# Block 0 in two halves on two queues, block 2 and K's weights moved up in the order of the first loads

## The chip, the cores and the metric

The kernel runs on one core of one Trainium2 chip. The time is device time of one execution in microseconds (us), and lower is better. A core has five engines that each run their own list of instructions in order: TensorE (PE: matmuls, and weight loads beside them), VectorE (DVE), ScalarE (ACT), GpSimd (POOL) and SyncE (SP). They wait for one another through semaphores. SP, ACT and POOL also issue DMA transfers, which the core's 16 DMA engines carry out.

## The reference

One input x of 2048 rows (tokens) by 512 columns goes through a layernorm without weights, and the result xn feeds two branches whose outputs are added to x. All tensors are bf16.

```python
def _A_ref(x, wqkv, wo):          # sliding local attention, 32 heads of 16
    qkv = (x @ wqkv).reshape(B, S, 3, H, Dh)   # -> q, k, v
    idx = pos[:, None] - off[None, :]          # 8 positions: s, s-2, ..., s-14
    logits = einsum('bhsd,bhswd->bhsw', q, k[idx]) * Dh ** -0.5   # masked where idx < 0
    o = einsum('bhsw,bhswd->bhsd', softmax(logits), v[idx])
    return o.reshape(B, S, D) @ wo

def _B_ref(x, w_in, w_sp, b_sp, w_out):        # gated MLP, mixed over positions
    z = gelu(x @ w_in)                         # 512 -> 1792
    z1, z2 = z[..., :896], layernorm(z[..., 896:])
    g = einsum('ts,bsf->btf', w_sp, z2) + b_sp[None, :, None]    # w_sp is 2048 x 2048
    return (z1 * g) @ w_out                    # 896 -> 512

xn = layernorm(A_x)
return A_x + _A_ref(xn, A_wqkv, A_wo) + _B_ref(xn, B_w_in, B_w_sp, B_b_sp, B_w_out)
```

## The kernel before

The 2048 rows are handled as 16 blocks of 128 rows, and for the wide matmuls as 4 groups of 512 rows. All tensors in SBUF are slices of one tile, `arena` (bf16), small statistics lie in `fpool` (f32), and PSUM is one tile, `ps`. So the profile names nearly every operand arena, fpool or ps, and the line number tells the operations apart.

**Stages on TensorE.** First come 15 matmuls on constants (`warm0` to `warm14`, line 561; eight of 512 columns and seven of 128), which need no data. Then V (line 666), the second half of B's first product, called z2 (line 770, in two halves of 448 columns), Q and K (line 682), z1 (line 813), g, the mix over positions with w_sp (line 910), a reduction for the logits (line 718), and the output blocks, attention part (line 966) and MLP part (line 975).

**The first blocks.** Blocks 0 and 1 don't wait for their layernorm: VectorE sums the row (`sum0`, line 592) and centres it (`cen0`, line 594), TensorE transposes the centred block (`xTc0_0`, `xTc0_1`, line 578), ACT copies it out of PSUM (line 599), and the factor 1/std (`rstd`, on POOL, line 621) is applied when V and z2 leave PSUM. The statistics (`bnst`, line 603; `bnag`, 605; `vpe`, 609) and the normalised block (`norm`, line 637) follow. Blocks 2 and 3 are normalised and then transposed on TensorE (`xTr`) with a copy on ACT (`xTe`, line 627). All other blocks, and blocks 0 and 1 for Q and K, are transposed by a DMA from `xn` (`xTd`, line 631, on SP). Q and K of the first group of 512 rows (`Q0_0`, `K0_0`, ...) read the transposed blocks 0 to 3.

**Loads.** ACT issues block 0 (`ldx0`, line 541), block 1 (line 514) and the first half of z2's weights for columns 0 to 447 (`ldwin2a0`, 224 KB, line 524). SP issues V's weights in two halves of 256 KB (`ldwv0`, `ldwv1`, line 518), `ldwin2a1` (224 KB), blocks 2 and 3 (128 KB each), `ldwin2b` (448 KB, line 530: z2's weights for the other columns), blocks 4 to 7, Q's weights (`ldq`, 512 KB, line 536), the DMA transposes `xTd0` and `xTd1`, K's weights (`ldk`, 512 KB, line 536), and blocks 8 to 15. A transpose waits on SP for its `norm`; what is behind it on SP waits too.

**What sets the order.** Every operation is a task with the engine, an estimated duration, priority, and what it reads and writes. `Plan.schedule` (line 123) is a list scheduler: it lays all tasks out in time by their estimates and so fixes each engine's list of instructions before the kernel is built. Semaphore waits are then set from reads and writes. Its settings are `tol` (how much later than the earliest task one of better priority may start and still be taken), the assumed DMA bandwidth and latency, `overlap` (subtracted from the time for which a VectorE task holds its engine), and `land`, a table with landing times in ns given for the first loads. All of these only steer the order; nothing at run time depends on them. In addition, lists of names (lines 1006 to 1015) force an order on the tasks named, so the start on TensorE, POOL, SP, VectorE and ACT is written out by hand:

```python
["ldq", "xTd0", "xTd1", "ldk"] + ["ldx%d" % b for b in range(8, NB)],     # SP
("rstd2", "rstd1", "rstd3", "rstd4", "Vw0"),                              # POOL
("sum0", "cen0", "sum1", "cen1", "bnst0", "bnag0", "vpe0", "bnst2", "bnag2", "vpe2", "bnst1",
 "bnag1", "vpe1", "norm2", "bnst3", "bnag3", "vpe3", "norm0", "norm1", "norm3", "bnst4"),   # VectorE
```

On TensorE the list is 12 warm-up matmuls, the transposes of block 0, three more warm-ups, then V0_0, the transposes of block 1, V0_1, V1, z2_0_0, z2_1_0, z2_0_1, xTr2, z2_1_1, V2, xTr3, z2_2, V3, z2_3, Q0_0.

Of the kernel before, what the change touches and what calls it, by code (L numbers as in the profile page):

```python
# [338 lines left out]
def build_kernel(nc, A_x, A_wqkv, A_wo, B_x, B_w_in, B_w_sp, B_b_sp, B_w_out, out, report=False, emit=True):  # L339
# [3 lines left out]
    NB = S // 128  # L343
# [5 lines left out]
    NVS = 4  # L349
    NPB = 3  # L350
    NXT = 4
    NWARM = 15
    x2 = A_x[0]
    o2 = out[0]

# [3 lines left out]
    off = {}  # L359
# [34 lines left out]
    plan = Plan()  # L394

    with ExitStack() as es:
        ar = es.enter_context(nc.sbuf_tensor("arena", [128, AR], BF))
# [4 lines left out]
        def A(name, n, o2_=0):  # L402
            return ar[:, off[name] + o2_: off[name] + o2_ + n]

        def AC(o_, dims):
            return bass.AP(tensor=ar, offset=o_, ap=[[AR, 128]] + [list(d) for d in dims])
# [10 lines left out]
        def P(bk, n, o_=0):  # L417
            return ps[:, bk.col(o_): bk.col(o_) + n]
# [73 lines left out]
        def dma(eng, fn, nbytes, chan, reads=(), writes=(), name="", xbar=False, prio=0.0, after=()):  # L492
            return T(eng, fn, reads=reads, writes=writes, name=name, prio=prio, after=after,
                     dma=dict(chan=chan, nbytes=nbytes, xbar=xbar))
# [12 lines left out]
          writes=["ident"], est=300, name="ident1")  # L507
# [4 lines left out]
        def ld_x(b, eng="sp"):  # L512
            sl = b
            return dma(eng, lambda e: e.dma_start(A("xin", 512, 512 * sl), x2[128 * b:128 * b + 128, :]), 128 * 512 * 2,
                ("xin", sl), writes=[("xin", sl)], name="ldx%d" % b)

        def ld_wv(hf):
            dma("sp", lambda e: e.dma_start(AC(off["wv"] + 1024 * hf, [[512, 2], [1, 512]]),  # L518
                                            A_wqkv[256 * hf:256 * hf + 256, 1024:1536].rearrange("(c p) n -> p c n",
                                                                                               p=128)),  # L520
                256 * 512 * 2, ("wv", hf), writes=[("wv", hf)], name="ldwv%d" % hf)

        def ld_win2a(kh, eng):
            dma(eng, lambda e: e.dma_start(
                AC(off["w_in2"] + 1792 * kh, [[896, 2], [1, 448]]),
                B_w_in[256 * kh:256 * kh + 256, 896:1344].rearrange("(c p) n -> p c n", p=128)),
                256 * 448 * 2, ("w_in2a", kh), writes=[("w_in2a", kh)], name="ldwin2a%d" % kh)
# [7 lines left out]
        def ld_wqk(which, eng):  # L535
# [2 lines left out]
                A_wqkv[:, 512 * which: 512 * which + 512].rearrange("(c p) n -> p c n", p=128)),  # L538
                512 * 512 * 2, ("wqk", which), writes=[("wqk", which)], name="ld%s" % ("qk"[which]))

        dma("act", lambda e: e.dma_start(A("xin", 512), x2[0:128, :]), 128 * 512 * 2, ("xin", 0),
            writes=[("xin0", 0), ("xin0", 1)], name="ldx0")
        ld_x(1, "act")
        ld_win2a(0, "act")
        ld_wv(0)
        ld_wv(1)
        ld_win2a(1, "sp")
        ld_x(2, "sp")
        ld_x(3, "sp")
        ld_win2b()  # L550
        ld_x(4, "sp")
# [5 lines left out]

        bw = plan.bank("warm")
        for wi in range(NWARM):
            n_ = 512 if wi < 8 else 128  # L560
            T("pe", (lambda bw, n_: lambda t: t.matmul(P(bw, n_), ones[:, 0:128], ones[:, 0:n_], start=True,
                                                       stop=True))(bw, n_),
              writes=[bw], est=(427.0 if n_ == 512 else 107.0), name="warm%d" % wi, prio=1000)

        T("act", lambda a: a.activation(Fv("prime", 4), mhalf, ACTF.Gelu_apprx_tanh), reads=["mhalf"],
          writes=["prime"], est=1500, name="actprime", tbl="gelu")
# [263 lines left out]
        for b in range(2, NB):  # L830
# [7 lines left out]
          writes=[("KTpad", c) for c in range(4)], est=170, name="ktpad", prio=2, after=lnr[:8])  # L838
# [164 lines left out]


        byname = {t.name: t for t in plan.tasks}
        for names in (["warm%d" % wi for wi in range(NWARM - 3)] + ["xTc0_0", "xTc0_1"] +
                      ["warm%d" % wi for wi in range(NWARM - 3, NWARM)] +
                      ["V0_0", "xTc1_0", "xTc1_1", "V0_1", "V1_0", "V1_1", "z2_0_0", "z2_1_0", "z2_0_1", "xTr2",
                       "z2_1_1", "V2_0", "V2_1", "xTr3", "z2_2_0", "z2_2_1", "V3_0", "V3_1", "z2_3_0", "z2_3_1", "Q0_0"],
                      ("rstd2", "rstd1", "rstd3", "rstd4", "Vw0"), ["ldq", "xTd0", "xTd1", "ldk"] + ["ldx%d" % b for b in range(8, NB)],  # L1010
                      ("sum0", "cen0", "sum1", "cen1", "bnst0", "bnag0", "vpe0", "bnst2", "bnag2", "vpe2", "bnst1",
                       "bnag1", "vpe1", "norm2", "bnst3", "bnag3", "vpe3", "norm0", "norm1", "norm3", "bnst4"),
                      ["bnst%d" % b for b in range(4, NB)],
                      ("xcT0_0", "xcT0_1", "xcT1_0", "xcT1_1", "Ve0", "xTe2", "Ve1", "z2g0", "xTe3", "z2g1", "Ve2", "z2g2",
                       "z2s0"), ("V10_1", "Q3_3"), ("z2_3_1", "Q0_1"), ("z2_3_1", "Q0_2"), ("z2_3_1", "Q0_3")):
            for n0, n1 in zip(names, names[1:]):
                if byname[n0] not in byname[n1].deps:
                    byname[n1].odeps.add(byname[n0])

        plan.schedule(tol=30.0, dma_bw=270.0, dma_lat=1300.0, overlap=0.0,  # L1020
                      land=dict(ldx0=3580.0, ldx1=4750.0, ldwv0=4100.0, ldwv1=5350.0, ldwin2a0=6550.0, ldwin2a1=6600.0, ldx2=7050.0, ldx3=7400.0,
                                ldwin2b=8650.0, ldx4=9050.0, ldx5=9400.0, ldx6=9750.0, ldx7=10200.0, ldq=11700.0,
                                ldk=15000.0))
        if report:
            print("arena", AR, "fp", FR)
            plan.report()
# [15 lines left out]
def bass_parallel_sum__sliding_local_dilated__mixer_gmlp__prompt_kernel(  # L1042
    nc, A_x, A_wqkv, A_wo, B_x, B_w_in, B_w_sp, B_b_sp, B_w_out, out
):
    build_kernel(nc, A_x, A_wqkv, A_wo, B_x, B_w_in, B_w_sp, B_b_sp, B_w_out, out)
# [28 lines left out]
```

## Time and profile before

| | us |
|---|---|
| median of 3 runs | 237.98 (237.9, 237.98, 239.03) |
| the profiled execution | 238.3 |
| its span, first to last instruction | 237.1 |
| PE busy | 231.5 (98%) |
| DVE busy | 215.8 (91%) |
| ACT busy | 95.2 (40%) |
| POOL busy | 32.1 (14%) |
| DMA, all 16 engines | 44.12 MB, 186 GB/s on average |

The profile is one execution, and its spans are in us from the first instruction. Busy times add up instructions; register, branch and DMA-issuing instructions are not counted. Matmuls overlap: one of 512 columns is shown with 379 ns, but they follow each other every 216 ns, so differences of start times are used where matmuls follow each other. Single matmul records can be missing. A few landing times of the first loads, as time of issue + time from issue to landing:

| load | issued | landed after |
|---|---|---|
| block 0 (ACT) | 0.81 | 2.7 |
| V's weights, halves (SP) | 0.80, 1.32 | 3.2, 4.0 |
| block 1 (ACT) | 1.26 | 3.1 |
| z2's weights, first columns (ACT, SP) | 1.74, 1.82 | 5.3, 5.4 |
| blocks 2, 3 (SP) | 2.33, 2.8 | 5.1, 4.9 |
| z2's weights, other columns (SP) | 3.31 | 5.7 |
| Q's weights (SP) | 6.21 | 5.7 |
| DMA transposes of blocks 0, 1 (SP) | 11.24, 12.6 | 2.9, 2.4 |
| K's weights (SP) | 13.88 | 4.5 |
| block 15 (SP) | 18.0 | 5.0 |

### The profile page before, as it was taken

Reading aid. Unit: us, or ns where it says so; the run is one execution under the profiler, and the core shown is the slowest. Engines: PE = TensorE matmul, PEld = TensorE weight load, DVE = VectorE, ACT = ScalarE, POOL = GpSimd, SP = SyncE. Lnnn points to the kernel's source line nnn. Section 1 sums busy time; section 2 is a strip of 40 time slices with the busy share of each in tenths; the row PEclk is TensorE's granted clock in tenths of the full one; section 3 lists DMA queues with packets and bytes.
Section 4 is the critical chain, followed back from the end, with each engine's and each line's share of the span. In section 5 each row is a group of like instructions: output and inputs, shape, how many; then the busy total and the mean of one; then the engine's idle time right before and its main releaser. Section 6 shows DMA issues by size and latency. Waiting matters only on the chain.

```text
span 237.1 us, 2958 instructions
## 1 busy us (share of the span) xinstructions
PE 231.5 (98%) x1109; PEld 108.5 (46%) x1130; DVE 215.8 (91%) x269; ACT 95.2 (40%) x141; POOL 32.1 (14%) x56
## 2 busy tenths in 40 slices
PE   8998999999999999999999999999999999999996
PEld 3444455555444444444444444444444444444443
DVE  4787989999997899999999999999989998999982
ACT  3496889988986896601113411111111111000000
POOL 1476381401634000000000000000000000000000
DMA  6979869998147239014299999999899866393443
GB/s 205 304 205 259 205 135 197 142 230 187 66 152 249 60 116 115 0 33 144 66 358 230 225 231 185 296 173 316 274 212 271 293 189 195 76 320 118 145 139 129
DMA packets 83117, 44.12 MB, mean 186 GB/s; under 512 B 55440, under 2 KB 82464, under 8 KB 83104
## 3 DMA queue, kind: packets, MB, share of 16 engines
q1 hardware_dynamic: 81600, 41.30, 70.7%
q0 software_dynamic: 800, 2.11, 2.3%
q10 hardware_dynamic: 704, 0.52, 0.7%
q8 instruction: 9, 0.15, 0.2%
q14 instruction: 4, 0.03, 0.1%
HBM read 26.35 MB, written 4.21 MB: 129 GB/s over the span
## 4 chain that ended last, share of the span: by engine, by line
PE 90%; DMA 4%; DVE 3%; issue 1%; SPq 1%; ACT 0%; POOL 0%; DVEq 0%
PE ps L910 41%; PE ps L682 11%; PE ps L813 10%; PE ps L975 10%; PE ps L770 8%; PE ps L966 6%; PE ps L666 4%; DMA arena<-in_A_x_dram 2%; DMA arena<-in_A_wqkv_dram 2%; DVE fpool L603 1%; ACT arena L775 0%; PE ps L718 0%; SPq L518 0%; DVE arena L981 0%; DVE fpool L605 0%
## 5 line engine op out<-in xcount | busy, mean ns | idle before, releaser
L910 PE MATMUL ps<-arena 128*128 128x512 bf16 x439 | 96.6, 379 | 0.5
L910 PEld LDWEIGHTS ps<-arena 128*128 128x128 bf16 x448 | 43.7, 98 | 53.1 <-issue 0.4
L918 ACT ACTIVATE arena<-ps 128x1024 bf16<-128x1024 f32 (+1 forms) x16 | 14.7, 916 | 75.3 <-PE ps L910 75.3
L703 DVE TENSOR_TENSOR arena<-arena 128x4096 bf16<-128x4096 bf16 x16 | 36.5, 2288 | 0.2
L938 DVE TENSOR_TENSOR arena<-arena 128x4096 bf16<-128x4096 bf16 x16 | 36.5, 2284 | 0.0
L941 DVE TENSOR_TENSOR arena<-arena 128x2048 bf16<-128x2048 bf16 (+1 forms) x32 | 30.6, 958 | 1.0
L682 PE MATMUL ps<-arena 128*128 128x512 bf16 x126 | 28.9, 379 | 1.3 <-DMA arena<-in_A_wqkv_dram 1.2
L708 DVE TENSOR_TENSOR arena<-arena 128x4096 bf16<-128x4096 bf16 x12 | 27.5, 2290 | 0.3
L975 PE MATMUL ps<-arena 128*128 128x512 bf16 (+2 forms) x117 | 26.9, 366 | 0.1
L770 PE MATMUL ps<-arena 128*128 128x448 bf16 x128 | 26.0, 352 | 0.0
L813 PE MATMUL ps<-arena 128*128 128x512 bf16 x110 | 24.4, 379 | 0.1
L682 PEld LDWEIGHTS ps<-arena 128*128 128x128 bf16 x128 | 14.3, 113 | 14.7 <-DMA arena<-in_A_wqkv_dram 1.7
L691 ACT ACTIVATE arena<-ps 128x1024 bf16<-128x1024 f32 x16 | 16.3, 1021 | 5.3 <-PE ps L682 5.0
L770 PEld LDWEIGHTS ps<-arena 128*128 128x128 bf16 x128 | 12.4, 98 | 11.7 <-DMA arena<-in_B_w_in_dram 0.2
L975 PEld LDWEIGHTS ps<-arena 128*128 128x128 bf16 x119 | 11.4, 98 | 12.8
L813 PEld LDWEIGHTS ps<-arena 128*128 128x128 bf16 x112 | 10.9, 98 | 13.3 <-ACT arena L819 0.3
L966 PE MATMUL ps<-arena 128*128 128x512 bf16 (+2 forms) x66 | 16.5, 366 | 0.1
L819 ACT ACTIVATE arena<-ps 128x1024 bf16<-128x1024 f32 (+1 forms) x16 | 13.9, 922 | 4.9 <-PE ps L813 4.9
L666 PE MATMUL ps<-arena 128*128 128x512 bf16 x60 | 15.2, 379 | 0.7 <-ACT arena L599 0.3
L780 ACT ACTIVATE arena<-arena 128x896 bf16<-128x896 bf16 x16 | 15.1, 946 | 0.1
L775 ACT ACTIVATE arena<-ps 128x896 bf16<-128x896 f32 x14 | 12.8, 915 | 3.3 <-PE ps L770 3.3
L981 DVE TENSOR_TENSOR arena<-ps,arena 128x512 bf16<-128x512 f32 (+2 forms) x17 | 10.4, 653 | 3.3 <-PE ps L975 2.8
(61 smaller groups left out, 168.8 us busy)
## 6 DMA issues: line engine op xcount, KB each, us to landing
arena<-vscr SPq DMA_DIRECT2D x16, 1024.0 KB, 6.0
arena<-in_A_x_dram SPq DMA_DIRECT2D x30, 128.0 KB, 4.1
vscr<-arena POOLq DMA_DIRECT2D x16, 128.0 KB, 2.3
out_dram<-arena SPq DMA_DIRECT2D x15, 128.0 KB, 2.0
arena<-in_A_wqkv_dram SPq DMA_DIRECT2D x2, 512.0 KB, 5.1
arena<-in_B_w_in_dram SPq DMA_DIRECT2D x1, 896.0 KB, 5.4
arena<-in_B_w_out_dram SPq DMA_DIRECT2D x1, 896.0 KB, 5.0
arena<-arena SPq DMA_TRANSPOSE x34, 2.9
```

The costliest lines, as they stand in the source:

```text
L666: last = t.matmul(P(bk, 512), xTv(b, dc), A("wv", 512, 512 * dc), start=(dc == 0), stop=(dc == 3))
L682: last = t.matmul(P(bk, 512, 512 * which), AC(off["wqk"] + 2048 * which + 512 * dc + c, [[4, 128]]), AC(off["xnT"] + dc * S + 512 * j, [[1 ...
L691: T("act", lambda a: a.activation(AC(qo, [[ko - qo, 2], [1, 512]]), P(bk, 1024).rearrange("p (t n) -> p t n", t=2), ACTF.Copy, scale=0.5), ...
L703: T("dve", (lambda pbv, qb, kb: lambda v: v.tensor_tensor(pbv, qb, kb, ALU.mult))(pbv, qb, kb), reads=rd, writes=[("pb", s_)], est=c_tt(40 ...
L708: T("dve", (lambda av, bv: lambda v: v.tensor_tensor(av, av, bv, ALU.add))(av, bv), reads=[("pb", 1)], writes=[("pb", acc)], est=c_tt(4096 ...
L770: last = t.matmul(P(bk, 448, 512 * hf), xTv(b, dc), AC(off["w_in2"] + 896 * dc + 448 * hf, [[1, 448]]), start=(dc == 0), stop=(dc == 3))
L813: last = t.matmul(P(bk, 512, 512 * i), AC(off["w_in1"] + 896 * dc + 128 * fc, [[1, 128]]), AC(off["xnT"] + dc * S + 512 * j, [[1, 512]]), ...
L910: last = t.matmul(P(bk, 512, 512 * i), AC(off["z2"] + FH * sh + 128 * fc, [[1, 128]]), AC(off["wT%d" % r_] + sh * 512, [[1, 512]]), start= ...
L938: T("dve", lambda v: v.tensor_tensor(tv, tv, av, ALU.mult), reads=[("attn", b)], writes=[("Vs", sv)], est=c_tt(4096), name="pv%d" % b, pri ...
L941: T("dve", (lambda n: lambda v: v.tensor_tensor(A("Vs", n, 4096 * sv), A("Vs", n, 4096 * sv), A("Vs", n, 4096 * sv + n), ALU.add))(n), wri ...
L966: last = t.matmul(P(bk, cn), AC(off["OT"] + 512 * tb + 128 * cc, [[1, 128]]), AC(off["wo"] + 512 * cc + c0, [[1, cn]]), start=(cc == 0), s ...
L975: last = t.matmul(P(bk, cn), AC(off["z1T"] + fc * S + 128 * tb, [[1, 128]]), AC(off["w_out"] + 512 * fc + c0, [[1, cn]]), start=False, sto ...
```

## The change

Block 0 is loaded by two DMAs of 64 rows each, one on ACT and one on SP, where SP's half is ahead of V's weights. Block 2's load moves ahead of `ldwin2a1` on SP. K's weights move ahead of the transposes `xTd0` and `xTd1`, directly behind Q's. `norm0` moves up on VectorE to just behind `vpe2`, and `rstd0` is written to the front of POOL's list. One of the wide warm-up matmuls goes (15 to 14, seven of 512 columns), and four instead of three of the narrow ones stand behind block 0's transposes, ten instead of twelve warm-ups ahead of them. The scheduler's settings change: `tol` 30 to 5, assumed bandwidth 270 to 250, latency 1300 to 1600, `overlap` 0 to 30, and the landing table. The computation is the same.

```diff
--- before.py
+++ after.py
@@ -349,7 +349,7 @@
     NVS = 4
     NPB = 3
     NXT = 4
-    NWARM = 15
+    NWARM = 14
     x2 = A_x[0]
     o2 = out[0]
 
@@ -538,14 +538,16 @@
                 A_wqkv[:, 512 * which: 512 * which + 512].rearrange("(c p) n -> p c n", p=128)),
                 512 * 512 * 2, ("wqk", which), writes=[("wqk", which)], name="ld%s" % ("qk"[which]))
 
-        dma("act", lambda e: e.dma_start(A("xin", 512), x2[0:128, :]), 128 * 512 * 2, ("xin", 0),
-            writes=[("xin0", 0), ("xin0", 1)], name="ldx0")
+        for hf, eng in ((0, "act"), (1, "sp")):
+            dma(eng, (lambda hf: lambda e: e.dma_start(ar[64 * hf:64 * hf + 64, off["xin"]: off["xin"] + 512],
+                                                       x2[64 * hf:64 * hf + 64, :]))(hf),
+                64 * 512 * 2, ("xin0", hf), writes=[("xin0", hf)], name="ldx0_%d" % hf)
         ld_x(1, "act")
         ld_win2a(0, "act")
         ld_wv(0)
         ld_wv(1)
+        ld_x(2, "sp")
         ld_win2a(1, "sp")
-        ld_x(2, "sp")
         ld_x(3, "sp")
         ld_win2b()
         ld_x(4, "sp")
@@ -557,7 +559,7 @@
 
         bw = plan.bank("warm")
         for wi in range(NWARM):
-            n_ = 512 if wi < 8 else 128
+            n_ = 512 if wi < 7 else 128
             T("pe", (lambda bw, n_: lambda t: t.matmul(P(bw, n_), ones[:, 0:128], ones[:, 0:n_], start=True,
                                                        stop=True))(bw, n_),
               writes=[bw], est=(427.0 if n_ == 512 else 107.0), name="warm%d" % wi, prio=1000)
@@ -1003,24 +1005,26 @@
 
 
         byname = {t.name: t for t in plan.tasks}
-        for names in (["warm%d" % wi for wi in range(NWARM - 3)] + ["xTc0_0", "xTc0_1"] +
-                      ["warm%d" % wi for wi in range(NWARM - 3, NWARM)] +
+        for names in (["warm%d" % wi for wi in range(NWARM - 4)] + ["xTc0_0", "xTc0_1"] +
+                      ["warm%d" % wi for wi in range(NWARM - 4, NWARM)] +
                       ["V0_0", "xTc1_0", "xTc1_1", "V0_1", "V1_0", "V1_1", "z2_0_0", "z2_1_0", "z2_0_1", "xTr2",
                        "z2_1_1", "V2_0", "V2_1", "xTr3", "z2_2_0", "z2_2_1", "V3_0", "V3_1", "z2_3_0", "z2_3_1", "Q0_0"],
-                      ("rstd2", "rstd1", "rstd3", "rstd4", "Vw0"), ["ldq", "xTd0", "xTd1", "ldk"] + ["ldx%d" % b for b in range(8, NB)],
-                      ("sum0", "cen0", "sum1", "cen1", "bnst0", "bnag0", "vpe0", "bnst2", "bnag2", "vpe2", "bnst1",
-                       "bnag1", "vpe1", "norm2", "bnst3", "bnag3", "vpe3", "norm0", "norm1", "norm3", "bnst4"),
+                      ("rstd0", "rstd2", "rstd1", "rstd3", "rstd4", "Vw0"),
+                      ["ldq", "ldk", "xTd0", "xTd1"] + ["ldx%d" % b for b in range(8, NB)],
+                      ("sum0", "cen0", "sum1", "cen1", "bnst0", "bnag0", "vpe0", "bnst2", "bnag2", "vpe2", "norm0",
+                       "bnst1", "bnag1", "vpe1", "norm2", "bnst3", "bnag3", "vpe3", "norm1", "norm3", "bnst4"),
                       ["bnst%d" % b for b in range(4, NB)],
-                      ("xcT0_0", "xcT0_1", "xcT1_0", "xcT1_1", "Ve0", "xTe2", "Ve1", "z2g0", "xTe3", "z2g1", "Ve2", "z2g2",
-                       "z2s0"), ("V10_1", "Q3_3"), ("z2_3_1", "Q0_1"), ("z2_3_1", "Q0_2"), ("z2_3_1", "Q0_3")):
+                      ("xcT0_0", "xcT0_1", "xcT1_0", "xcT1_1", "Ve0", "xTe2", "Ve1", "z2g0", "xTe3",
+                       "z2g1", "Ve2", "z2g2", "z2s0"), ("V10_1", "Q3_3"), ("z2_3_1", "Q0_1"), ("z2_3_1", "Q0_2"),
+                      ("z2_3_1", "Q0_3")):
             for n0, n1 in zip(names, names[1:]):
                 if byname[n0] not in byname[n1].deps:
                     byname[n1].odeps.add(byname[n0])
 
-        plan.schedule(tol=30.0, dma_bw=270.0, dma_lat=1300.0, overlap=0.0,
-                      land=dict(ldx0=3580.0, ldx1=4750.0, ldwv0=4100.0, ldwv1=5350.0, ldwin2a0=6550.0, ldwin2a1=6600.0, ldx2=7050.0, ldx3=7400.0,
-                                ldwin2b=8650.0, ldx4=9050.0, ldx5=9400.0, ldx6=9750.0, ldx7=10200.0, ldq=11700.0,
-                                ldk=15000.0))
+        plan.schedule(tol=5.0, dma_bw=250.0, dma_lat=1600.0, overlap=30.0,
+                      land=dict(ldx0_0=2700.0, ldx0_1=3050.0, ldx1=3650.0, ldwv0=4350.0, ldwv1=5250.0, ldwin2a0=6300.0,
+                                ldwin2a1=6850.0, ldx2=5800.0, ldx3=7250.0, ldwin2b=8400.0, ldx4=8750.0, ldx5=9100.0,
+                                ldx6=9450.0, ldx7=9800.0, ldq=11300.0, ldk=12800.0))
         if report:
             print("arena", AR, "fp", FR)
             plan.report()
```

## The prediction

> **What bounds the kernel now.** I read the busy line and the chain of the page first, then TensorE's waits, then the timeline of the first 19 us on every engine, then the landing times of single loads, and last the tail.
>
> The busy line, the chain by engine, and two of TensorE's five waits:
>
> ```profile
> PE 231.5 (98%) x1109; PEld 108.5 (46%) x1130; DVE 215.8 (91%) x269; ACT 95.2 (40%) x141; POOL 32.1 (14%) x56
> PE 90%; DMA 4%; DVE 3%; issue 1%; SPq 1%; ACT 0%; POOL 0%; DVEq 0%
> ...
> PE ps L682 <- DMA arena<-in_A_wqkv_dram: 1.2, 1, 1.2
> ...
> PE ps L666 <- ACT arena L599: 0.3, 1, 0.3
> ```
>
> TensorE is the bound: 231.5 of 237.1 us. Its waits sum to 2.7 us, 0.8 of them before the first matmul. One is large: 1.2 us for K's weights (line 682 is the Q and K projections). After that, only 0.2 us is called a wait. So time comes only from this wait, from starting V earlier, or from new stalls.
>
> The first 19 us, from the timelines (start, length, engine, line, operation, count; in brackets the idle time before and what ended it):
>
> ```profile
> 0.80 0.97 SPq L518 DMA_DIRECT2D arena<-in_A_wqkv_dram  x2
> 0.81 0.42 ACTq L541 DMA_DIRECT2D arena<-in_A_x_dram  x1
> 3.50 0.69 DVE L592 TENSOR_REDUCE fpool<-arena 128x1 f32<-128x512 bf16 x1 [2.31 <-DMA arena<-in_A_x_dram]
> 5.56 0.59 PE L666 MATMUL ps<-arena 128*128 128x512 bf16 x2 [0.28 <-ACT arena L599]
> 7.46 0.69 DVE L603 BATCH_NORM_STATS2 fpool<-arena 128x6 f32<-128x512 bf16 x1 [0.89 <-DMA arena<-in_A_x_dram]
> 7.62 2.43 PE L770 MATMUL ps<-arena 128*128 128x448 bf16 x12
> 9.03 0.58 PEld L770 LDWEIGHTS ps<-arena 128*128 128x128 bf16 x4 [0.18 <-DMA arena<-in_B_w_in_dram]
> 11.24 2.59 SPq L631 DMA_TRANSPOSE arena<-arena  x2
> 13.88 0.58 SPq L536 DMA_DIRECT2D arena<-in_A_wqkv_dram  x1
> 16.25 1.03 PE L682 MATMUL ps<-arena 128*128 128x512 bf16 x4
> 18.45 6.24 PE L682 MATMUL ps<-arena 128*128 128x512 bf16 x27 [1.18 <-DMA arena<-in_A_wqkv_dram]
> 18.74 0.69 DVE L603 BATCH_NORM_STATS2 fpool<-arena 128x6 f32<-128x512 bf16 x1 [1.53 <-DMA arena<-in_A_x_dram]
> ```
>
> Block 0's sum starts at 3.50, V at 5.56, z2 at 7.62. SP's last early load (Q's weights) is issued at 6.21 for 0.43; then SP stands until norm0 lets the first transpose go at 11.24. Only behind both transposes (2.59) does it issue K's weights, at 13.88; they land 4.5 later. Q0_0 runs from 16.25 to 17.28, and TensorE then stands 1.18.
>
> The tail, from the chain and SP's timeline:
>
> ```profile
> 228.75 1.19 SPq L947 DMA_TRANSPOSE arena<-arena  x1
> ...
> 232.76 0.65 PE ps L966 x4
> ```
>
> The last transpose of the attention output is issued at 228.75 and lands 2.45 later (such transposes took 2.4 to 2.5), at 231.2. The block that reads it starts at about 232.6. So VectorE's chain has 1.4 us to spare at the end.
>
> **The change part by part.**
>
> K's weights ahead of the first transposes. They go out at about 7.2 instead of 13.88 (Q's 6.21, plus the extra 0.48 slot on SP, plus 0.5). Q's 512 KB landed at 11.9 (5.7 after issue), and the four loads and Q's ahead of that moved at some 350 GB/s, so another 512 KB takes 1.5 more: K lands near 13.4, against a need at 17.2. The whole 1.18 goes. What is late next: Q0_0 needs both first transposes. In the old order they landed at 14.1 and 15.0 (2.9 and 2.4 after issue). Now their 2 x 1.29 us of issue stands behind one issue of about 0.5, which ends by 7.8, before norm0 is done; their data stands behind K's in the rings. The nearest row: the later transposes at 18.56 and 19.8 landed 5.1 and 4.3 after issue, 0.7 and 1.1 behind the eight loads ahead of them (the last landed at 23.0). By that the first two land at 14.1 and about 14.5 or, if norm1 is no earlier than before, at 15.0. Q0_0 needs them at 16.1, so 1 us is left. Cost 0; without that cover every us late is a us lost.
>
> Loads of blocks 8 to 15 follow the second transpose with no K issue between: 0.6 to 2 us sooner than 14.50. VectorE's 1.53 for block 8 shrinks; TensorE does not wait for it, so 0. But QK1 needs transposes 4 to 7, and the last (issued 23.2, landed 26.1) came just before TensorE's 26.22. Those four follow block 15's load on SP and move forward with it; if that is by only 0.6, 0.6 of the gain is lost there. I take the larger figure, since block 8's load no longer waits for K's issue (0.6) and norm0 and its 1.29 of transpose issue come early.
>
> Block 0 in halves. By the quarter-microsecond windows the engines had moved 127 KB by 2.50 and 256 KB by 3.00; both x0 (128 KB) and V's first weights (256 KB) were out at 0.8, and x0 landed at 3.50, some 0.5 after its share. Alone at the front, its 128 KB would be moved by about 2.5 and land near 3.05 to 3.1. So sum, centring, the first PE transposes and V start 0.42 sooner: 5.14, and V ends at 7.2 instead of 7.62. One warm-up matmul of 0.43 goes; the ten ahead of the transposes end at 0.84 + 7 x 0.427 + 3 x 0.11 = 4.16, in time for 4.3.
>
> But z2 then meets its weights. Their halves landed at 7.05 and 7.17; SP's half now has 128 KB of block 2 ahead (0.4 at 337 GB/s) and an issue 0.96 later: 7.2 to 7.55. z2_0_0 and z2_1_0 take 8 x 0.189 = 1.51, to 8.7 to 9.06. The second half of the weights (w_in2b) landed at 9.02, with 1,920 KB in all through it; the same 1,920 KB stand there after the change. So z2_0_1 starts at 9.02 to 9.06 instead of 9.13. The start is worth **-0.1**, the 0.42 is swallowed. Bounds: the engines' gaps between 2.0 and 2.75 (shares 0.63, 0.82, 0.57) and at 4.5 to 5.0 come to 0.35 us; filled, w_in2b lands by that much earlier: -0.45. If instead landing follows issue, which is 0.48 later for everything behind the half on SP, w_in2b lands at 9.5: +0.37. I take -0.1, because the shares near 1.0 from 2.75 to 10 say bytes set the pace.
>
> DVE and POOL orders. norm0 (0.40) moves ahead of bnst1 and norm2. norm2 ended at 9.88 for a transpose on PE at 9.94. Block 2 lands about 1 us earlier, so the statistics that waited 0.89 at 7.46 start near 6.5, and norm2 ends near 9.5 even with norm0 ahead. rstd0 heads POOL as it did in the trace (6.73). Cost 0; if block 2 came no earlier, 0.4 would go.
>
> New constants for the list scheduler can reorder everything behind. A gain is bounded by the idle left on PE after 18.45, about 0.3; a loss by VectorE slipping (below). With a single wait of 0.2 in 216 us under the old constants, I take 0.
>
> **Sum:** -1.18 - 0.1 = -1.28. The profiled execution took 238.3 (span 237.1 and 1.2 around it); it becomes 237.0 with a span of 235.8. The median of the runs is 0.32 below the profiled one, so 237.98 - 1.28 = **236.7**. With the start's bounds, 236.3 to 237.2. About 0.5% (1.19 us, so 236.8 and 239.2) is what can be told from no change here.
>
> **The rivals.**
>
> The halves buy nothing and cost the slot (w_in2b at 9.5): -1.18 + 0.37 = -0.8, **237.2**. For it: wv0 and every load behind it is issued 0.48 later. Against: the saturated shares. The Trainium skill, DMA: Bandwidth & Descriptors, section Rules for kernel authors, speaks for it: two transfers to disjoint partition halves share the same engines and serialize, so one 128-partition transfer should be used. By that rule alone x0 would land at 3.50 as before; what the trace shows is only that x0 shared the engines with wv0.
>
> The start is kept (w_in2b 0.35 earlier): -1.18 - 0.45 = -1.6, **236.35**. For it: the gaps at 2.0 to 2.75. Against: the loads behind the first need an issue of 0.45 to 0.48 each, and only 128 KB are out at 0.8 instead of 384.
>
> The transposes behind K's weights come late, and Q0_0 or QK1 waits. It decides beyond 1 us late; 1.3 more takes the whole gain: **238.0**. For it: 26.1 against 26.22 at QK1, and a transpose issue that took 2.05 at 21.1 beside loads. Against: all that is ahead of them on SP ends earlier.
>
> Slower: the new order makes VectorE late for TensorE. VectorE is 91% busy; its 269 operations are now each counted 30 ns shorter, 8 us in all, and it has 1.4 us to spare at the end, when both chains move by the same amount. One 4096-wide product (2.28) put ahead of block 15's chain takes 0.9 of the gain; slower by 0.5% needs 1.4 + 1.28 + 1.19 = 3.9. A block's whole chain (2.28 + 1.95 + 0.43 = 4.66) costs 4.66 - 1.4 - 1.28: +2.0, **240.0**. Against: VectorE waited only 6 to 7 us after 18.6, mostly for ACT, PE and loads that move too.
>
> **How the numbers follow.** Forecast 0.46 (236.5 to 237.0, of that 0.28 beyond 0.5%); halves cost 0.14 (same); start kept 0.13 (faster); transposes late 0.08 (same); VectorE late 0.19 (slower). Faster 0.28 + 0.13 = 0.41; same 0.18 + 0.14 + 0.08 = 0.40; slower 0.19. The range starts at 235.9 (the start kept, the 0.3 of idle gone, and the 0.1 by which the two lower runs differ) and reaches to 239.4, halfway into the last case, so that about 0.12 is left out. Cases of both signs hold chance; the forecast's own range is 236.3 to 237.2.
>
> **What would show it.** Block 0's sum near 3.1; V near 5.15; z2_0_1 still at 9.0 to 9.1, with TensorE's wait for w_in now visible; K's weights issued near 7.2 and landed by 13.5; Q0_0 near 16.1 and K right behind it without idle; block 8's load issued near 12.4. It is wrong if Q0_0 waits for a transpose, if z2_0_0 starts after 7.7, or if the waits of TensorE after 20 us, 0.2 now, exceed 1 us (lines 718, 966 and 975 are where VectorE could be late).

## The result and the profile after

| | before | after |
|---|---|---|
| median, us (22 runs each) | 238.06 (237.6 to 239.03) | 237.03 (236.63 to 239.47) |
| after / before | | 0.9959, 95% interval 0.9948 to 0.9971 |
| the profiled execution, us | 238.3 | 236.64 |
| its span, us | 237.1 | 235.4 |

The change gains 0.98 us (238.06 x 0.0041; by the interval 0.7 to 1.2). The interval excludes zero, but the gain is below the 0.5% (1.19 us) under which the prediction counts a time as unchanged. The two profiled executions differ by more, 1.66 us, because the one of after is among the quickest of its kernel and the one of before is 0.24 above its median.

From the page of after, the busy line and the chain by engine:

```profile
PE 232.0 (99%) x1129; PEld 108.5 (46%) x1129; DVE 208.0 (88%) x269; ACT 94.7 (40%) x141; POOL 34.6 (15%) x56
PE 96%; DMA 2%; DVE 1%; ACTq 0%; issue 0%; DVEq 0%
```

All of TensorE's waits in after (engine, line, what it waited for, us in total, times, longest):

```profile
PE ps L563 <- PEq L1063: 0.8, 1, 0.8
PE ps L580 <- DVE arena L596: 0.3, 1, 0.3
PE ps L668 <- ACT arena L601: 0.2, 1, 0.2
```

K's wait of 1.2 us is gone, and none has come in its place: all three lie ahead of the first V matmul. The chain is now 96% TensorE. VectorE counts 7.8 us less for the same 269 operations.

The start and the end of after, from the timelines (columns as in the prediction; where a view ends inside a row of matmuls, its last line counts only those up to there):

```profile
0.80 0.58 SPq L542 DMA_DIRECT2D arena<-in_A_x_dram  x1
0.81 0.57 ACTq L542 DMA_DIRECT2D arena<-in_A_x_dram  x1
1.43 0.84 ACTq L514 DMA_DIRECT2D arena<-in_A_x_dram  x1
3.39 0.69 DVE L594 TENSOR_REDUCE fpool<-arena 128x1 f32<-128x512 bf16 x1 [2.19 <-DMA arena<-in_A_x_dram]
5.01 0.69 DVE L594 TENSOR_REDUCE fpool<-arena 128x1 f32<-128x512 bf16 x1 [0.55 <-DMA arena<-in_A_x_dram]
5.45 0.59 PE L668 MATMUL ps<-arena 128*128 128x512 bf16 x2 [0.22 <-ACT arena L601]
6.51 0.98 SPq L536 DMA_DIRECT2D arena<-in_A_wqkv_dram  x2
7.78 2.43 PE L772 MATMUL ps<-arena 128*128 128x448 bf16 x12
8.45 3.86 SPq L633 DMA_TRANSPOSE arena<-arena  x2
12.35 4.03 SPq L514 DMA_DIRECT2D arena<-in_A_x_dram  x8
16.11 7.07 PE L684 MATMUL ps<-arena 128*128 128x512 bf16 x32
23.02 2.43 PE L772 MATMUL ps<-arena 128*128 128x448 bf16 x12
25.29 4.91 PE L684 MATMUL ps<-arena 128*128 128x512 bf16 x22
...
221.10 1.19 SPq L949 DMA_TRANSPOSE arena<-arena  x1
```

Block 0's two halves are issued at 0.80 and 0.81, each for longer than the whole block was before (0.42). Q and K go out together from 6.51. Q0_0 starts at 16.11 and K follows as one piece of 32 matmuls. Then come **12** z2 matmuls, where before has 8, and the next group's Q and K (called QK1 from here on) at 25.29. The last transpose of the attention output goes out at 221.1 instead of 228.75. Two lines of before from the same view, not shown yet:

```profile
24.52 1.68 PE L770 MATMUL ps<-arena 128*128 128x448 bf16 x8
26.22 1.03 PE L682 MATMUL ps<-arena 128*128 128x512 bf16 x4
```

**One account for all kernels.** Matmuls overlap, so I count starts. From Q0_0 to the z2 behind it takes 8.27 us before (16.25 to 24.52) and 6.91 after (16.11 to 23.02): K's wait cost 1.36, not the 1.18 that is marked as idle. A z2 matmul takes 0.189, so QK1 could start 1.51 behind the eight of before; it starts 1.70 behind, 0.19 lost and not marked as a wait. After takes 2.27 for its 12, which is 12 x 0.189: nothing lost. Together 1.55 is gained behind Q0_0. The profiled time minus the start of Q0_0 says the same, 222.05 before and 220.53 after, 1.52 less. Here is that account for every kernel that ran (us; "K" is Q0_0 to z2 less 6.91, "QK1" the excess over 0.189 a matmul):

| kernel | Q0_0 starts | lost at K | lost at QK1 | profiled time less Q0_0's start | median | ratio to before |
|---|---|---|---|---|---|---|
| before | 16.25 | 1.36 | 0.19 | 222.05 | 238.06 | |
| after | 16.11 | 0 | 0 | 220.53 | 237.03 | 0.9959 |
| e1 | 16.02 | 0 | 0.87 | 221.35 | 237.78 | 0.9973 [0.9958, 0.9987] |
| e2 | 16.01 | 0 | 0 | 220.52 | 236.67 | 0.9934 [0.9919, 0.9949] |
| e3 | 16.37 | 0 | 0 | 220.53 | 236.89 | 0.9955 [0.9936, 0.9974] |
| e4 | 16.24 | 0 | 0 | 221.80 | 238.33 | 1.0009 [0.9995, 1.0022] |
| e5 | 16.81 | 0 | 0 | 220.68 | 237.17 | 0.9962 [0.9947, 0.9977] |
| e6 | 16.45 | 1.27 | 0.43 | 222.21 | 238.57 | 1.0016 [1.0007, 1.0025] |
| e7 | 16.33 | 0 | 0.57 | 221.10 | 237.49 | 0.9983 [0.997, 0.9997] |
| e8 | 16.22 | 0 | 0 | 220.80 | 237.17 | 0.996 [0.9948, 0.9972] |
| e9 | 16.41 | 0.78 | 0.68 | 222.04 | 237.39 | 0.9976 [0.996, 0.9991] |
| e10 | 16.30 | 0 | 0 | 220.57 | 236.94 | 0.996 [0.9948, 0.9973] |
| e11 | 16.00 | 0 | 0 | 220.50 | 236.69 | 0.9946 [0.9934, 0.9958] |
| e12 | 16.08 | 0 | 0 | 220.53 | 236.81 | 0.9952 [0.994, 0.9965] |

Six of the kernels without a stall behind Q0_0 agree within 0.07 in the fifth column, and before, e1, e6, e7 and e9 come within 0.05 of 220.53 when the losses of the two columns ahead of it are taken off. e4, e5 and e8 don't fit that. Part of it lies outside the span: in all 25 runs of these three the time is 1.39 to 1.54 above the span, in every run of the other kernels whose span is on record 1.17 to 1.35. Span less Q0_0's start is 219.29 in after and e5, 219.28 in e8 and 220.36 in e4, so e5 and e8 lose nothing inside it and e4 has a loss of its own, of 1.07 (below). Why these three kernels have more outside the span stays open. Ratios are against runs of before beside them, whose medians were 238.2 (e1 to e4), 238.08 (e5 to e8) and 237.85 (e9 to e12).

### The profile page after: what moved, and what is told of

It reads as the page before. It is cut to its first block, busy times and chain, and to the rows that moved or that the text cites. A ratio compares the mean times of both kernels' runs of the same rounds, so it can differ in the third digit from the quotient of the medians.

```text
span 235.4 us, 2986 instructions
## 1 busy us (share of the span) xinstructions
PE 232.0 (99%) x1129; PEld 108.5 (46%) x1129; DVE 208.0 (88%) x269; ACT 94.7 (40%) x141; POOL 34.6 (15%) x56
## 4 chain that ended last, share of the span: by engine, by line
PE 96%; DMA 2%; DVE 1%; ACTq 0%; issue 0%; DVEq 0%
PE ps L912 41%; PE ps L684 12%; PE ps L772 10%; PE ps L815 10%; PE ps L977 10%; PE ps L968 6%; PE ps L668 6%; DMA arena<-in_A_x_dram 2%; PE ps L720 1%; DVE arena L983 0%; PE ps L580 0%; DVE fpool L594 0%; ACTq L542 0%; DVE arena L596 0%; DVEq L319 0%
## 5 line engine op out<-in xcount | busy, mean ns | idle before, releaser
L684 PEld LDWEIGHTS ps<-arena 128*128 128x128 bf16 x128 | 14.4, 113 | 13.2 <-ACT arena L672 0.4
L983 DVE TENSOR_TENSOR arena<-ps,arena 128x512 bf16<-128x512 f32 (+2 forms) x17 | 11.1, 658 | 9.1 <-PE ps L977 8.7
L923 DVE TENSOR_TENSOR arena<-arena 128x1024 bf16<-128x1024 bf16 (+1 forms) x16 | 10.0, 623 | 9.3 <-ACT arena L920 9.2
L772 PEld LDWEIGHTS ps<-arena 128*128 128x128 bf16 x128 | 12.4, 98 | 11.7
```

The source lines that it names most:

```text
L684: last = t.matmul(P(bk, 512, 512 * which), AC(off["wqk"] + 2048 * which + 512 * dc + c, [[4, 128]]), AC(off["xnT"] + dc * S + 512 * j, [[1 ...
L772: last = t.matmul(P(bk, 448, 512 * hf), xTv(b, dc), AC(off["w_in2"] + 896 * dc + 448 * hf, [[1, 448]]), start=(dc == 0), stop=(dc == 3))
```

## The experiments

In all but e4 to e8 the orders of the base kernel are kept and only the tasks named are moved, by editing each engine's planned list. In e4 to e8 changed settings lay the plan out anew. No kernel leaves work out. `...` in an edit stands for lines left out, which only number the tasks anew or define `behind`, a helper that puts one task directly behind another on its engine.

**e1: K's weights first, alone.** Before, with one task moved on SP.

```diff
+        sp_ = plan.order["sp"]
+        lk = byname["ldk"]
+        sp_.remove(lk)
+        sp_.insert(sp_.index(byname["ldq"]) + 1, lk)
...
```

> The kernel before with one move: K's weights are issued directly behind Q's, ahead of the two transposes; every other engine keeps its order of before. Theory (the gain of the change is K's wait): K0_0 follows Q0_0 without idle, and as Q0_0's first matmul to z2 of block 4 took 8.27 us before and 6.91 after, 1.2 to 1.35 us go: 236.7 to 236.9 against 238.06. The first transpose still waits for norm0 at 11.2, so block 8's load is issued at about 13.9. Rival (the halves or the new order carry at least half of the gain): 0.5 us or less, 237.5 or more.

Measured: 237.78, ratio 0.9973: about half of what was expected (three of its twelve runs, 236.67 to 236.76, came as expected). K's wait is gone, but TensorE stands one step later. From e1's waits of TensorE:

```profile
PE ps L682 <- DMA arena<-arena: 0.7, 1, 0.7
```

And from its timelines of TensorE, then SP:

```profile
16.02 7.07 PE L682 MATMUL ps<-arena 128*128 128x512 bf16 x32
22.93 1.68 PE L770 MATMUL ps<-arena 128*128 128x448 bf16 x8
25.31 1.03 PE L682 MATMUL ps<-arena 128*128 128x512 bf16 x4 [0.70 <-DMA arena<-arena]
...
10.87 2.65 SPq L631 DMA_TRANSPOSE arena<-arena  x2
13.56 5.30 SPq L514 DMA_DIRECT2D arena<-in_A_x_dram  x8
18.91 5.12 SPq L631 DMA_TRANSPOSE arena<-arena  x4
```

Transposes 4 to 7 are issued from 18.91. TensorE now reaches the z2 ahead of QK1 1.59 sooner (22.93 against 24.52), and QK1 waits for the last of them: 2.38 between starts where 1.51 would do. Of the 1.36 won at K, 0.87 - 0.19 goes here. Moving K's weights is therefore not the whole change.

**e2: the change without the halves.** After, with block 0 whole on ACT and no half on SP.

```diff
+        byname["ldx0_0"].fn = lambda e: e.dma_start(A("xin", 512), x2[0:128, :])
+        gone = byname["ldx0_1"]
+        plan.order["sp"].remove(gone)
+        plan.tasks.remove(gone)
+        for t in plan.tasks:
+            t.deps.discard(gone)
+            t.odeps.discard(gone)
```

> The changed kernel with block 0 in one DMA on ACT; every engine's order as after, only SP's half is gone. Theory (the halves are worth nothing): block 0's sum starts at 3.4 to 3.5 instead of 3.39, block 1 lands at 4.4 to 4.6 instead of 5.0, V starts within 0.15 us of 5.45, z2 starts earlier than 7.78; time as after within 0.2 us (237.0). Rival (the halves are the start's gain): V starts 0.4 later or more, and the time goes up by 0.3 or more, 237.3 to 237.5.

Measured: 236.67, ratio 0.9934, not slower without them; the time is 0.4 below after's, where 0.2 either way was expected. The start of e2 by its timeline:

```profile
0.80 0.43 ACTq L1028 DMA_DIRECT2D arena<-in_A_x_dram  x1
1.26 0.45 ACTq L514 DMA_DIRECT2D arena<-in_A_x_dram  x1
3.56 0.69 DVE L594 TENSOR_REDUCE fpool<-arena 128x1 f32<-128x512 bf16 x1 [2.37 <-DMA arena<-in_A_x_dram]
4.65 0.69 DVE L594 TENSOR_REDUCE fpool<-arena 128x1 f32<-128x512 bf16 x1
5.62 0.59 PE L668 MATMUL ps<-arena 128*128 128x512 bf16 x2 [0.22 <-ACT arena L601]
7.67 2.43 PE L772 MATMUL ps<-arena 128*128 128x448 bf16 x12
```

Whole, block 0 is summed 0.17 later than in after (3.56, a little past the 3.4 to 3.5 expected), but block 1's sum starts 0.36 sooner, so V starts 0.17 later and z2 0.11 earlier. Q0_0 starts 0.10 earlier.

**e3: K's weights back behind the transposes.** After, with `ldk` moved behind `xTd1`.

```diff
+        sp_ = plan.order["sp"]
+        lk = byname["ldk"]
+        sp_.remove(lk)
+        sp_.insert(sp_.index(byname["xTd1"]) + 1, lk)
...
```

> The changed kernel with K's weights issued behind both transposes again; every other engine's order as after. Theory (what counts is only whether K lands before about 17.0): the second transpose's issue ends at 12.3 because norm0 and norm1 are early now, K's weights go out at 12.35 and land 4.5 later at 16.8, just in time: no wait or up to 0.2 us, 236.9 to 237.3. Rival (the place behind the transposes is what costs): K waits about 1.2 again and the time is 238.0 to 238.3.

Measured: 236.89, ratio 0.9955, as after. With `norm0` early both transposes are issued from 8.56, K's weights go out at 12.45 instead of 13.88 and land 4.3 later, at 16.8, in time. So within after's order, the early `norm0` is enough to bring K's weights in time, here about 0.5 us ahead of need; in before's order it was not in the one trace there is (e9).

**e4: the old settings.** After, with the scheduler's old settings; lists and landing table stay new.

```diff
-        plan.schedule(tol=5.0, dma_bw=250.0, dma_lat=1600.0, overlap=30.0,
+        plan.schedule(tol=30.0, dma_bw=270.0, dma_lat=1300.0, overlap=0.0,
```

> The changed kernel with the scheduler's settings of before (tol 30, bandwidth 270, latency 1300, overlap 0); loads and lists of names as after. Theory (the order behind the start is worth nothing while TensorE never waits): within 0.3 us of after, 236.8 to 237.3; VectorE has less to spare at the end (some 1 to 2 us). Rival (the new settings carry part of the gain): 237.5 or more, with waits of TensorE after 20 us.

Measured: 238.33, ratio 1.0009: the whole gain is lost, against 0.9955 of e3, which ran beside it, though K doesn't wait. The theory fell, and the rival held. From e4's waits of TensorE:

```profile
PE ps L968 <- DMA arena<-arena: 0.9, 1, 0.9
```

And from its timelines near the end, VectorE's three lines first, then one of SP and one of TensorE:

```profile
220.63 1.88 DVE L983 TENSOR_TENSOR arena<-ps,arena 128x512 bf16<-128x512 f32 x3
224.21 0.69 DVE L983 TENSOR_TENSOR arena<-ps,arena 128x512 bf16<-128x512 f32 x1 [1.70 <-PE ps L977]
224.82 2.28 DVE L940 TENSOR_TENSOR arena<-arena 128x4096 bf16<-128x4096 bf16 x1
...
229.57 1.19 SPq L949 DMA_TRANSPOSE arena<-arena  x1
...
232.09 0.82 PE L968 MATMUL ps<-arena 128*128 128x384 bf16 x4 [0.89 <-DMA arena<-arena]
```

VectorE stands 1.70 in its own queue for an output add (line 983, the add of block 11, `fin11_0`) that needs TensorE's result, and the chain of block 15 stands behind it. Its transpose goes out at 229.57, and TensorE's first block that reads it starts 2.57 after the matmuls ahead of it instead of 1.51: 1.06 of the 1.27 that e4 has over after in the table (the rest lies outside the span).

**e5, e6, e7: which setting?** I took `overlap`. e5 is after with `overlap` 0 (the first pair of lines); e6 is before with `overlap` 30 (the second pair); e7 is e6 with e1's move.

```diff
-        plan.schedule(tol=5.0, dma_bw=250.0, dma_lat=1600.0, overlap=30.0,
+        plan.schedule(tol=5.0, dma_bw=250.0, dma_lat=1600.0, overlap=0.0,
...
-        plan.schedule(tol=30.0, dma_bw=270.0, dma_lat=1300.0, overlap=0.0,
+        plan.schedule(tol=30.0, dma_bw=270.0, dma_lat=1300.0, overlap=30.0,
```

> The changed kernel with one setting of before, overlap 0 instead of 30; the other settings stay. Theory (the overlap setting alone decides at the end: with 0 the scheduler puts output adds that wait for TensorE ahead of the last steps of block 15's attention chain, and TensorE then waits for that chain): VectorE about 215 us busy again, TensorE waits 0.5 to 1 us at line 968 near 231, 237.6 to 238.3. Rival (it is tol, or the assumed bandwidth and latency): 236.8 to 237.2, no wait at line 968.

> The kernel before with overlap 30 instead of 0, nothing else. Theory (the order behind the start is worth something only where TensorE gets there earlier): K's wait stays at about 1.2, VectorE about 208 us busy and done with block 15's chain some 10 us sooner, but the time moves by 0.3 us at most: 237.8 to 238.2. Rival (the better order of VectorE's list is worth the gain by itself): 237.3 or less.

> The kernel before with both: K's weights ahead of the first transposes, and overlap 30. K first alone gave 0.5 to 0.6 us. Theory (K's wait of 1.34 us goes, part of it is lost again at QK1 behind the transposes of blocks 4 to 7, since norm0 is as late as before, and part at the end, where the old order makes TensorE wait for VectorE): the part at the end comes back; 236.9 to 237.4, a wait of up to 0.7 at line 682 stays. Rival (nothing was lost at the end, the runs of K first alone differ for another reason): 237.7 to 237.9.

Measured: e5 237.17 (0.9962), no wait at line 968, and VectorE at 207.9 us: `overlap` alone isn't it, that theory fell. e6 238.57 (1.0016): VectorE's busy time drops from 215.8 to 207.7 us and the time doesn't drop at all, with K's wait still there; it is even 0.4 longer, a little more than expected. e7 237.49 (0.9983), just above its theory's range: no tail wait, but 0.41 marked at QK1 (0.57 between starts). The account says that e1 had lost nothing at the tail either (221.35 less its 0.87 at QK1 is 220.48); the loss under the old order sits at QK1.

**e8: the one add, with the old settings.** e4 with `fin11_0` moved on VectorE behind the chain of block 15. On SP the store and the load that hang on that add go behind the transpose.

```diff
...
+        behind("dve", "fin11_0", "pvc15")
+        behind("sp", "ldxr15", "OTd15")
+        behind("sp", "st11_0", "OTd15")
...
```

> The changed kernel with all the settings of before, as in the run that took 238.3, and by hand one output add (block 11) moved on VectorE from ahead of block 15's product to behind block 15's chain, with its store and the load of block 15's x moved behind block 15's transpose on SP. Theory (this one add, which waits 1.7 us for TensorE, makes the whole difference): no wait at line 968, 237.0 to 237.4. Rival (the old settings cost elsewhere, or VectorE has too much work as such): 237.9 or more.

Measured: 237.17, ratio 0.996, as after, and no wait at line 968. e8's VectorE timeline where e4 waited:

```profile
220.60 1.88 DVE L983 TENSOR_TENSOR arena<-ps,arena 128x512 bf16<-128x512 f32 x3
222.40 2.28 DVE L940 TENSOR_TENSOR arena<-arena 128x4096 bf16<-128x4096 bf16 x1
```

The product follows the three adds at once, 2.42 sooner. One 0.69-us operation in the wrong place had cost e4 its gain. SP's order was not what held e4's transpose: it went out at 229.57, when VectorE's chain had just ended (229.12 + 0.43).

**e9, e10: `norm0` early, alone and taken back.** e9 is before with `norm0` directly behind `vpe2` on VectorE (the first line); e10 is after with `norm0` back behind `vpe3` (the second).

```diff
...
+        behind("dve", "norm0", "vpe2")
...
+        behind("dve", "norm0", "vpe3")
...
```

> The kernel before with one move on VectorE: norm0 directly behind vpe2. Loads, SP's list (K's weights behind both transposes), settings and all else as before. Theory (norm0, late, holds SP: it decides when everything behind the first transpose goes out): first transpose at about 8.2, second at about 11.2, K's weights at 12.5 and landed by 16.9, block 8's load at 13.1, so K0_0 waits 0.2 us at most and QK1 little: 236.8 to 237.3. Rival (K's place in SP's list is what counts): K0_0 still waits 0.8 or more, 237.6 or more.

> The changed kernel with norm0 moved back on VectorE to behind vpe3; K's weights stay ahead of the transposes. Theory (as above): no wait for K, but the first transpose at about 11, block 8's load at about 13.8, transposes 4 to 7 about 1.5 later than in the changed kernel, and QK1 waits 0.4 to 1.2 for the last of them: 237.5 to 238.0. Rival (with K ahead, norm0's place is free): 237.0, no wait at line 684.

Measured: e9 237.39 (0.9976), between theory and rival and about what e1 gains. In its trace K's weights go out at 12.64, but land only 5.3 later, at 17.9. e9's waits:

```profile
PE ps L682 <- DMA arena<-in_A_wqkv_dram: 0.6, 1, 0.6
PE ps L682 <- ACT arena L780: 0.5, 1, 0.5
```

That execution took 238.45, the longest of its eight runs (from 236.81), so the row shows what can still go wrong there, not the usual size. e10 236.94 (0.996): no stall, although its transposes stand as late as e1's; its theory fell, and the rival held. e10's timelines of SP and TensorE:

```profile
10.79 2.60 SPq L633 DMA_TRANSPOSE arena<-arena  x2
...
18.68 5.37 SPq L633 DMA_TRANSPOSE arena<-arena  x4
...
23.21 2.43 PE L772 MATMUL ps<-arena 128*128 128x448 bf16 x12
25.48 4.70 PE L684 MATMUL ps<-arena 128*128 128x512 bf16 x21
```

Against e1's 18.91 the second set of transposes is only 0.23 sooner, and Q0_0 is 0.28 later; the larger part of e10's cover is that 12 z2 matmuls instead of 8 stand ahead of QK1, 0.76 us. The 12 come with the new tolerance, bandwidth and latency: all seven kernels planned with these have them, e5 with `overlap` 0 too, and the other seven have 8.

**e11, e12: the halves once more.** e11 is e2's kernel (its edit in short below) and e12 is after without an edit, one beside the other.

```diff
+        byname["ldx0_0"].fn = lambda e: e.dma_start(A("xin", 512), x2[0:128, :])
+        gone = byname["ldx0_1"]
+        plan.order["sp"].remove(gone)
...
```

> The changed kernel with block 0 in one DMA, a second time, beside the changed kernel on the same chip. Theory (two DMAs of 64 rows cost issue time and put block 1 0.4 later): 0.2 to 0.4 us shorter than the changed kernel, 236.6 to 236.8. Rival (they cost nothing, the first run's difference was scatter): within 0.1 us of it.

> The changed kernel itself, as it was: 236.9 to 237.2. Block 0's two issues 0.57 to 0.58 us each and block 1's 0.84, as in the three profiles of kernels with the halves so far; the start of V between 5.45 and 5.7.

Measured: 236.69 (0.9946) and 236.81 (0.9952). The difference is 0.12 us, less than the theory's 0.2, and the intervals overlap. By the medians of all their runs, after and e12 stand at 237.03 and 236.81, e2 and e11 at 236.67 and 236.69: the halves cost 0.1 to 0.4 us or nothing, and no gain from them shows. The quickest version that ran is the change without them.

## Why the prediction came out as it did

Forecast -1.28, measured -0.98, inside the forecast's own range; the time of 237.03 is 0.3 above the 236.7. The main term was right. One of the forecast's three signs of being wrong did come, though: z2_0_0 started at 7.78, after 7.7. The other two did not: Q0_0 waited for no transpose, and TensorE has no marked wait after 20 us.

**K's wait: right, and mis-sized.** "The whole 1.18 goes": it went, and gave 1.36, since idle time that is counted from modelled ends of overlapping matmuls leaves out a part of the slots that pass empty (a matmul is shown with 379 ns, its slot is 216, and 1.18 + 0.16 is 1.34). Another 0.19 went at QK1, where I had read only that the last transpose "came just before TensorE's 26.22"; start to start it was a small loss already. So 1.52 came behind Q0_0 where I had 1.18.

**What comes next behind K: right in the trace.** K's weights were issued at 7.0 and landed at 13.5 (forecast near 7.2 and by 13.5). The transposes landed at 13.95 and 14.4 (forecast 14.1 and 14.5), Q0_0 started at 16.11, and block 8's load was issued at 12.35 (forecast 12.4). The rival that the transposes come late did not happen in after. But its place, QK1, was the right one to look at: with K moved alone (e1) it takes half the gain.

**Block 0 in halves: wrong.** The step that failed is "Alone at the front, its 128 KB would be moved by about 2.5 and land near 3.05 to 3.1". The sum started at 3.39, 0.11 sooner instead of 0.42. I had counted bytes and one extra issue of 0.48 on SP. By the windows of after, the engines had moved only 57 KB by 2.50 and 126 KB by 2.75, where before had 127 KB by 2.50; SP's half landed at 2.9, but ACT's, which the sum needs too, at 3.3. The trace shows the halves' issues at 0.58 and 0.57, and the next on ACT, block 1, at 0.84 instead of 0.46. Block 1 landed at 5.0 instead of 4.36, so V started 0.11 sooner but z2 0.16 later, at 7.78. The cap that I had put on this gain, z2's second weights at 9.02, never came to bear: they landed at 8.96, and z2_0_1 needed them at 7.78 + 8 x 0.189 = 9.29. (The gaps that I added up to 0.35 us for the bound of -0.45 come to 0.31 by the shares of their windows.)

The rival "the halves buy nothing" holds for the halves, by another road than the one priced: the delay came through block 1, not through w_in2b at 9.5. The Trainium skill, DMA: Bandwidth & Descriptors, section Rules for kernel authors, advises one 128-partition transfer instead of two to disjoint partition halves. The runs agree as far as they can tell: with one transfer z2 starts at 7.67 in e2 and e11, against 7.78 in after and 7.75 in e12, and the medians are 236.67 and 236.69 against 237.03 and 236.81.

**The start: -0.1 held in the profile, by luck.** Q0_0 started 0.14 sooner in the profiled run, but not by the forecast's road, since z2 started 0.16 later. In after and eight others of the fourteen kernels Q0_0 follows z2's start by 8.33 to 8.34; in before it took 8.63, as TensorE's weight loads for the transposes of blocks 2 and 3 stood for VectorE's normalised blocks:

```profile
9.94 0.23 PEld L578 LDWEIGHTS ps<-arena 128*128 128x128 bf16 x4 [0.33 <-DVE arena L637]
...
12.12 0.23 PEld L578 LDWEIGHTS ps<-arena 128*128 128x128 bf16 x4 [0.55 <-DVE arena L637]
```

That isn't the change's doing either: e1 has before's loads and orders up to there, except that K's weights follow Q's at once, and in its trace Q0_0 follows z2 by 8.33 and starts at 16.02, sooner than in after; e9, which has the early `norm0`, still shows 8.72. In the seven kernels with halves Q0_0 starts between 16.08 and 16.81 (mean 16.30), in the seven without between 16.00 and 16.45 (mean 16.21). So no gain at the start is shown.

Why the medians gained 1.0 where the part behind Q0_0 gained 1.52 in the two traces stays open. If the remainders of 222.05 and 220.53 were fixed, the medians would put Q0_0 at 16.0 before and 16.5 after. But before's is not fixed: K's first matmul goes by when K's weights land, so that a later Q0_0 loses less there (e6 starts Q0_0 0.20 later than before and loses 1.27 instead of 1.36 at K).

**`norm0`, `rstd0`: cost 0 was right, use 0 was not said.** Block 2 landed 0.8 sooner (6.66 against 7.4) and its normalisation ended at 9.76, before its transpose at 10.05. What I had left out is that the early `norm0` is a second way to K's gain: within after's order e3 has it without K's move, e10 has K's move without it, and both take the same time as after. In before's order each of the two alone gives about half (e9 0.9976, e1 0.9973).

**Settings at 0: nothing is left over for them in the sum, but the reason did not hold.** "With a single wait of 0.2 in 216 us under the old constants, I take 0." But a TensorE that comes sooner needs an order that serves it sooner. Before's own order gives half of the gain back at QK1 (e1), and the old settings, planned with the new lists, give all of it back at the tail (e4). The slower rival named this engine and this place, block 15's chain at the end. It had another operation in mind, a product put ahead of the chain instead of an add that waits for TensorE, and it had the sign of the settings the wrong way round. The new ones take the risk away: that transpose now goes out 7.65 us sooner, and the output adds directly ahead of the last chain, three in before and four in e4, stand inside or behind it in after's timeline. The 1.4 us "to spare at the end" was no safe cover either, since the two chains did not move by the same amount: in e4 TensorE could have started that block at 231.03, 1.56 sooner than in before, while VectorE's product starts 0.83 later (224.82 against 223.99), because it stands behind the add that waits. Together that is 2.39 against 1.4, about the 1.06 lost.

**Open.** Which of tolerance, bandwidth and latency gives the new tail order is not settled: it appears with `overlap` 0 in e5 and with the three old values in e6. The cost of the halves is known only as 0 to 0.4 us. The spread of e1's runs (236.67 to 238.08) was not traced. The variation of Q0_0's start among kernels with the same loads (16.08 to 16.81) goes for the most part with z2's start (7.75 to 8.38 in the kernels with halves), which is seen but not explained. Block 2's earlier load, the front place of `rstd0` and the warm-up matmuls were not tried alone.

## What to carry to other kernels

Size a stall by the starts of the matmuls around it, and then look up the next thing that TensorE will reach sooner: here the transposes for QK1 and the last attention block, where half or all of the gain was given back. On an engine that runs in order, look for an operation that waits for TensorE and stands ahead of a chain that TensorE needs; one such add cost more than 1 us, though its engine stood idle meanwhile. Splitting a small first load over two queues has to be priced by the issues behind it, not by its bytes.

## What was not expected of the hardware

**Two half-size loads issued side by side.** With 64-row halves issued on SP and ACT at 0.80, each took 0.55 to 0.59 us, where block 0's whole load, issued on ACT at the same moment as V's weights on SP, took 0.41 to 0.43. One of the two queues then had a long issue: block 1's on ACT took 0.84 to 0.85 in after, e3, e4, e5 and e12. In e8 and e10 ACT's took 0.58 and 0.59, and the two V weights on SP 1.33 together instead of 1.08; there TensorE waited 0.4 to 0.5 for V's weights.

**A product overlaps an independent neighbour.** On VectorE, an output add starts 2.20 us after a 2.28-us product (203.24 to 205.44 in after), while the sum that reads the product starts 2.31 after it (205.06 to 207.37 in before). The lengths of the same 269 operations add up to nearly the same (225.9 us in before, 225.1 in after, by the groups' means), but with more such neighbours they overlap more and count 208.0 instead of 215.8 us. By itself that is worth nothing in time here (e6).
